# Dummy products from the start, activation tables regrouped in the first unit, and set-up writes moved, in a fused attention and gated feed-forward kernel

## The chip, the core and the metric

The kernel runs on one core of a Trainium2 chip. A core has TensorE (PE, matrix products into PSUM), VectorE (DVE), ScalarE (ACT, activation functions by tables), GpSimd (POOL) and SyncE (SP), and DMA queues. In this kernel GpSimd issues nearly all loads, and SyncE the stores. The metric is the device time of one execution in microseconds. Before the change it is 282.56 us, the median of three runs (282.09 to 282.75).

## What is computed

Two layers, one after the other. The first is an attention over 4 batches, 8 heads, 768 positions and head dimension 64, in which a query sees its neighbours nearer than 16 positions and one summary key for each block of 32:

```python
k_sum = k.reshape(B, H, nb, block, D).max(axis=3)
v_sum = v.reshape(B, H, nb, block, D).mean(axis=3)
scores_l = scale * np.matmul(q, k.transpose(0, 1, 3, 2))      # masked to |i - j| < 16
scores_s = scale * np.einsum('bhsd,bhnd->bhsn', q, k_sum) + np.log(block)
a = softmax(concatenate([scores_l_m, scores_s]))
x = a @ concatenate([v, v_sum])
```

The second layer takes x as 3072 tokens of 512, with d_ff = 1536:

```python
gelu = 0.5 * g * (1.0 + erf(g * inv_sqrt2))      # g = x @ w_gate
ffn_out = gelu * (x @ w_val) @ w_out
res_gate = 1.0 / (1.0 + np.exp(-(x @ w_res)))
out = x + res_gate * ffn_out
```

## The kernel before

**Units.** The work is cut into eight units (NU) of 384 tokens, two for each batch. For a unit, attention runs in four head pairs (hp):

- `s_step` (L268): 12 score products into the only buffer of the PSUM pool `ps_s`; exp on ScalarE (L280); a mask product on VectorE (L283), giving P.
- `av_step` (L286): 12 products of P with `vext` (v, and in partitions 96 to 127 the block means of v); a reciprocal and a product on VectorE give xn (L298, L300).
- `xt_step` (L302): three transposes on TensorE and a copy, giving xT (L307).

The feed-forward part of a unit follows:

- `fo_step` (L327), 12 times: four gate products (g) and four value products (vv) of 384 columns, gelu on ScalarE (L321), a product on VectorE giving gvT (L322). g and vv take PSUM buffers of `ps_mm`, which has four.
- `res_step` (L334), three times: four products of 512 columns and a tanh (L341).
- `ffn_step` (L343): 12 products of 512 columns for each of three sub-blocks, in pieces of four; `end_step` (L360) does two VectorE instructions (L354, L356) and the store.

While a unit's `res_step` and `ffn_step` run, the attention of the next unit is woven in by hand: `first_out` (L434) does it for unit 0, `mid_out` for the units after it. Each engine executes its instructions in the order in which the program lists them[...].

**Tables.** [...] Exp and tanh share one, gelu is in another; a load is put ahead of the activation that needs the other table. Copies need no change.

**The start.** `load_qk` (L85) brings k in two halves, `load_q` (L95) q, `v_loads` (L108) v in 12 windows, then the weights in pieces (L183 to L193), all by GpSimd in that order. VectorE writes constants in the meantime: `ident`, `maskt`, `bpair`, `bias_t`, `vext_consts`, `kw_consts`, `own_keys`, and `warm`, a tile of zeros. The program of unit 0 begins at L374. `k_step` turns k by 16 transposes for each head pair, copies it (L221) and takes block maxima on VectorE (`k_blocks`, L204). `q_step` (L228) turns q by eight transposes and a copy (L235). `vsum_mm` (L238) sums v over blocks with products of 256 columns that fill 32 columns of the array; the sums are cast (L392, L393) and copied into `vext` (`vsum_head`, L245). Then come the four `av_step`s and `xt_step`s of unit 0, with five dummy products between them (`keep_warm`, L403, a 128x128 by 512 product of zeros whose result nobody reads), and the first two gate and value products by hand (L418 to L431).

**Around L515.** In unit 0 the four `q_step`s of the batch's second half follow feed-forward steps 8 to 11. After step 10 the first score step of unit 1 is issued, whose exp falls on ScalarE between the gelus of steps 10 and 11.

The softmax here doesn't subtract the row's maximum and nothing guards it: scores larger than these inputs give would overflow.

## Time and profile before

| what | value |
|---|---|
| time | 282.56 us |
| span of the profiled execution | 281.2 us |
| TensorE busy | 260.4 us (93%) |
| VectorE busy | 163.5 us (58%) |
| ScalarE busy | 131.9 us (47%) |
| GpSimd busy | 103.3 us (37%) |
| gelu, 96 times | 47.0 us, 491 ns each |
| exp, 32 times | 28.8 us, 901 ns each |
| TensorE busy from 0 to 5, 5 to 10, 10 to 15 us | 0.00, 2.88, 3.92 us |
| TensorE busy from 40 to 45, 45 to 50 us | 4.29, 2.96 us |

Busy time is what an engine spent in instructions, not counting the issue of transfers. Products on TensorE overlap, and their ends are modelled, so its busy time is not its time at peak. The averages hide the stages. The last two rows of the table show what to look for: stretches in which the engine that is otherwise full stands still. An engine's idle time matters only where it lies on the chain of waits that ends last.

### The profile page before, as it was taken

To read this page: it belongs to the slowest core of one execution; us is meant where nothing else is said; L and a number is where in the kernel's file an instruction comes from. 1 tells how busy PE (TensorE), PEld (TensorE's weight loads), DVE (VectorE), ACT (ScalarE), POOL (GpSimd) and SP (SyncE) were. 2 spreads that over 40 slices of the span, in tenths; PEclk is the share of its full clock that TensorE was granted. 3 is DMA by queue.
4 is the path that set the end of the run, shared out by engine and by line. 5 is a ranking of instruction groups with operands and counts; after the bars stand their busy time and mean duration, and the time that the engine had idled before them with its cause. 6 is when DMAs were issued, how large, how long until landed. Compare 5 with 4: busy or idle time off the path is not lost.

```text
span 281.2 us, 5757 instructions
## 1 busy us (share of the span) xinstructions
PE 260.4 (93%) x2326; PEld 144.2 (51%) x2349; DVE 163.5 (58%) x366; ACT 131.9 (47%) x205; POOL 103.3 (37%) x130
## 2 busy tenths in 40 slices
PE   0799996999999999999899999999899999999994
PEld 0555553455555556455454555455455555456543
DVE  5965432489636734486866834575956733684424
ACT  1855549556473553652353434543254435444320
POOL 7995753600199982000899830000700000000000
PEclk9999999999999999999999999999999999999999
DMA  6999999991019999961099999421001100010003
GB/s 89 171 178 196 197 206 208 151 198 54 4 10 127 182 171 152 151 98 65 3 100 131 196 166 150 94 77 41 2 0 40 75 2 0 37 41 37 2 0 113
DMA packets 99818, 27.51 MB, mean 98 GB/s; under 512 B 83720, under 2 KB 96848, under 8 KB 99792
## 3 DMA queue, kind: packets, MB, share of 16 engines
q0 software_dynamic: 80560, 16.85, 68.4%
q1 hardware_dynamic: 19232, 10.30, 17.1%
q8 instruction: 18, 0.29, 0.4%
q14 instruction: 8, 0.07, 0.1%
HBM read 33.69 MB, written 6.29 MB: 142 GB/s over the span
## 4 chain that ended last, share of the span: by engine, by line
PE 83%; DVE 6%; ACT 4%; issue 3%; DMA 3%; POOL 0%; POOLq 0%; DVEq 0%
PE f L348 21%; PE g L316 20%; PE vv L316 19%; PE r L338 7%; PE ao L294 4%; PE s L276 3%; DMA q_sb<-in_q_dram 3%; PE xp L305 3%; DVE ks L207 2%; PE vs L241 2%; PE tp L233 2%; DVE gvT L322 2%; PE f L369 1%; ACT L280 1%; ACT L321 1%
## 5 line engine op out<-in xcount | busy, mean ns | idle before, releaser
L322 DVE TENSOR_TENSOR gvT<-ge,vv 128x384 bf16<-128x384 f32 x96 | 52.6, 552 | 58.9 <-PE vv L316 54.8
L321 ACT ACTIVATE ge<-g 128x384 f32<-128x384 f32 x96 | 47.0, 491 | 82.2 <-DVE gvT L322 43.7
L316 PE MATMUL vv<-xT,w_val 128*128 128x384 bf16 x384 | 78.4, 326 | 2.7 <-DVE gvT L322 2.7
L316 PE MATMUL g<-xT,w_gate 128*128 128x384 bf16 x384 | 79.9, 326 | 0.4 <-ACT ge L321 0.4
L348 PE MATMUL f<-w_out,gvT 128*128 128x512 bf16 x262 | 62.7, 379 | 1.4 <-issue 1.0
L316 PEld LDWEIGHTS <-w_val 128*128 128x128 bf16 x384 | 37.5, 98 | 28.7 <-issue 4.6
L316 PEld LDWEIGHTS <-w_gate 128*128 128x128 bf16 x384 | 35.8, 98 | 25.2 <-issue 3.0
L266 POOL COPY vext<-vsum 32x1536 bf16<-32x1536 bf16 x14 | 20.0, 1464 | 76.6 <-DMA vsum<-vpart 76.6
L280 ACT ACTIVATE P<-s,bias_t 128x768 bf16<-128x768 f32 x32 | 28.8, 901 | 30.6 <-PE s L276 30.5
L111 POOL DMA_DIRECT2D vext<-in_v_dram x48 | 36.5, 790 | 15.7 <-DMA w_out<-in_moe_w_out_dram 5.4
L348 PEld LDWEIGHTS <-gvT 128*128 128x128 bf16 x276 | 26.1, 98 | 29.1
L283 DVE TENSOR_TENSOR P<-P,maskt 128x768 bf16<-128x768 bf16 x32 | 17.7, 556 | 21.6 <-ACT P L280 21.6
L338 PE MATMUL r<-w_res,xT 128*128 128x512 bf16 x88 | 23.9, 381 | 0.4
L354 DVE SCALAR_TENSOR_TENSOR th<-th,f 128x512 f32<-128x512 f32 (+1 forms) x25 | 16.5, 659 | 6.4 <-PE f L348 6.1
L300 DVE TENSOR_TENSOR xn<-ao,rz 128x384 bf16<-128x384 f32 x32 | 17.8, 558 | 1.1
L119 POOL DMA_DIRECT2D k_nat<-in_k_dram x24 | 18.1, 771 | 0.0
L356 DVE SCALAR_TENSOR_TENSOR o<-th,xn 128x512 f32<-128x512 f32 (+1 forms) x25 | 16.8, 671 | 0.9
L298 DVE RECIPROCAL rz<-ao 128x6 f32<-128x6 f32 x32 | 6.2, 193 | 17.7 <-PE ao L294 17.7
L294 PEld LDWEIGHTS <-P 128*64 128x64 bf16 x384 | 9.0, 115 | 14.1 <-DVE P L283 5.5
L341 ACT ACTIVATE th<-r 128x512 f32<-128x512 f32 x24 | 14.2, 595 | 3.3 <-PE r L338 2.9
L207 DVE TENSOR_REDUCE ks<-kW 128x24 bf16<-128x768 bf16 x16 | 15.2, 948 | 0.3
L276 PE MATMUL s<-qT,kW 64*128 64x64 bf16 x384 | 11.8, 197 | 2.7 <-ACT P L280 2.7
(69 smaller groups left out, 188.4 us busy)
## 6 DMA issues: line engine op xcount, KB each, us to landing
out_dram<-o SPq DMA_DIRECT2D x23, 256.0 KB
vext<-in_v_dram POOLq DMA_DIRECT2D x40, 96.0 KB, 6.0
k_nat<-in_k_dram POOLq DMA_DIRECT2D x20, 96.0 KB, 3.7
q_sb<-in_q_dram POOLq DMA_DIRECT2D x4, 384.0 KB, 7.3
w_gate<-in_moe_w_gate_dram POOLq DMA_DIRECT2D x6, 256.0 KB, 8.2
w_val<-in_moe_w_val_dram POOLq DMA_DIRECT2D x6, 256.0 KB, 9.3
w_out<-in_moe_w_out_dram POOLq DMA_DIRECT2D x3, 512.0 KB, 14.3
q_nat<-in_q_dram POOLq DMA_DIRECT2D x12, 128.0 KB, 5.2
```

What stands on the lines that cost most here:

```text
L111: nc.gpsimd.dma_start(out=vext[b % 2][r0:r1, t, :, 0:D], in_=src)
L119: nc.gpsimd.dma_start(out=k_nat[r0:r0 + hi - lo, t].rearrange("p (h d) -> p h d", d=D), in_=k[b, :, lo:hi, :].rearrange("h p d -> p h d"))
L207: nc.vector.tensor_reduce(out=ks.rearrange("d (t n) -> d t n", n=2), in_=kw[:, :, WIN:WIN + QT].rearrange("d t (n w) -> d t n w", w=BLK), ...
L266: eng.tensor_copy(vext[b % 2][96:128, lo:hi, :, 0:D], src)
L276: nc.tensor.matmul(s[:, hh, t * QT:(t + 1) * QT], kw[ps, tt, hp, :], qt[ps, tt // 2, hp, (tt % 2) * QT:(tt % 2 + 1) * QT], start=True, sto ...
L280: nc.scalar.activation(P.rearrange("p a t q -> p a (t q)"), s[:, :, 0:TU], AF.Exp, scale=scale, bias=bias_t[:])
L294: nc.tensor.matmul(ao[64 * e:64 * e + 64, sub, hh, :], P[:, hh, t, :], vext[b % 2][:, half * HT + t, 2 * hp + hh, 0:D + 1], start=True, st ...
L316: nc.tensor.matmul(ps[:, 0:TU], w[:, ko, fo * 128:(fo + 1) * 128], st["xT"][:, ko, :], start=(ko == 0), stop=(ko == KO - 1), skip_group_ch ...
L321: nc.scalar.activation(ge[:], g[:, 0:TU], AF.Gelu)
L322: nc.vector.tensor_mul(gvT[:, fo, :], ge[:], vv[:, 0:TU])
L338: nc.tensor.matmul(r[:], st["xT"][:, ko, ss], w_res[:, ko, :], start=(ko == 0), stop=(ko == KO - 1))
L348: nc.tensor.matmul(st["f", sub][:], gvT[:, fo, ss], w_out[:, fo, :], start=(fo == 0), stop=(fo == FO - 1), skip_group_check=True)
```

## The change

It has four parts.

1. `keep_warm` now takes its buffer from `ps_s` and is called before any data has come (12 products), and three more times among the turns of k and q (3, 4 and 2). The memset of `warm` becomes VectorE's first instruction. The purpose is to have TensorE's clock up when the first real products come.
2. A gelu of one element (`gate1`) follows the fourth exp of unit 0. It has no use but to have the gelu table loaded there, and not at the first real gelu.
3. The score step of unit 1 after feed-forward step 10 is gone; `first_out` does it itself, and its order is new, so that no exp stands between gelus.
4. The constants for the second buffers (`vsum[1]`, `bgrp`, the ends of `k_nat`, `kW[1]`) are written after unit 0's attention and not at the start.

```diff
+    gate1 = const.tile([1, 1], F32, name="gate1")
...
+        nc.vector.memset(warm[:], 0.0)
         nc.vector.memset(ident[:], 0.0)
...
         own_keys(bmat, NT)
-        nc.vector.memset(warm[:], 0.0)
         vext_consts(1)
-        nc.vector.memset(vsum[1][96:128, :], 0.0)
-        own_keys(bgrp, 3)
-        nc.vector.memset(k_nat[0:32, 0], 0.0)
-        nc.vector.memset(k_nat[64:96, NT - 1], 0.0)
-        kw_consts(1)
...
-        for hp in range(3):
-            k_step(0, hp, ps_mm, "mm")
+        def keep_warm(n):
+            wp = ps_s.tile([128, 2, 512], F32, tag="s", name="wp")
+            for _ in range(n):
+                nc.tensor.matmul(wp[:, 0], warm[:, 0:128], warm[:], start=True, stop=True)
+
+        keep_warm(12)
+        k_step(0, 0, ps_mm, "mm")
+        k_step(0, 1, ps_mm, "mm")
+        keep_warm(3)
+        k_step(0, 2, ps_mm, "mm")
         tp3 = turn_pair(k_sb[0], 3, ps_mm, "mm")
+        keep_warm(4)
         q_step(0, 0, 0, ps_mm, "mm")
         k_place(0, 3, tp3)
+        keep_warm(2)
         q_step(0, 0, 1, ps_mm, "mm")
...
         s_step(0, 3, st)
+        nc.scalar.activation(gate1[:], bias_t[0:1, :], AF.Gelu)
         vsum_mm(0, vs, 8, NT)
...
         xt_step(0, 2, st, ps_t, "t", nc.scalar.copy)
+        nc.vector.memset(vsum[1][96:128, :], 0.0)
+        own_keys(bgrp, 3)
+        nc.vector.memset(k_nat[0:32, 0], 0.0)
+        nc.vector.memset(k_nat[64:96, NT - 1], 0.0)
+        kw_consts(1)
...
         def first_out(u, st, gvT, nst):
-            s_step(n, 1, nst)
+            s_step(n, 0, nst)
             res_step(st, 0)
             res_step(st, 1)
+            ffn_step(st, gvT, 0, 0, 4)
+            ffn_step(st, gvT, 1, 0, 4)
             av_step(n, 0, nst)
+            s_step(n, 1, nst)
+            res_step(st, 2)
+            ffn_step(st, gvT, 2, 0, 4)
+            ffn_step(st, gvT, 0, 4, 8)
+            av_step(n, 1, nst)
             s_step(n, 2, nst)
-            res_step(st, 2)
-            for sub in range(NSUB):
-                ffn_step(st, gvT, sub, 0, 4)
-            av_step(n, 1, nst)
+            xt_step(n, 0, nst, **turn)
+            ffn_step(st, gvT, 1, 4, 8)
+            ffn_step(st, gvT, 2, 4, 8)
+            av_step(n, 2, nst)
             s_step(n, 3, nst)
-            xt_step(n, 0, nst, **turn)
-            ffn_step(st, gvT, 0, 4, 8)
-            ffn_step(st, gvT, 1, 4, 8)
-            av_step(n, 2, nst)
             xt_step(n, 1, nst, **turn)
-            ffn_step(st, gvT, 2, 4, 8)
+            ffn_step(st, gvT, 0, 8, FO)
+            end_step(u, st, 0)
+            ffn_step(st, gvT, 1, 8, FO)
             av_step(n, 3, nst)
             xt_step(n, 2, nst, **turn)
-            ffn_step(st, gvT, 0, 8, FO)
-            end_step(u, st, 0)
+            ffn_step(st, gvT, 2, 8, FO)
             xt_step(n, 3, nst, **turn)
-            ffn_step(st, gvT, 1, 8, FO)
             end_step(u, st, 1)
-            ffn_step(st, gvT, 2, 8, FO)
             end_step(u, st, 2)
...
-                if u == 0 and fo == 10:
-                    nst = new_unit()
-                    s_step(1, 0, nst)
```

## The prediction

> **What bounds the kernel now.** First the summary of the chain that ended last, for the engine that carries the span; then that chain in order of time, to find where TensorE does not carry it; then the timeline there. The summary:

> ```profile
> PE 83%; DVE 6%; ACT 4%; issue 3%; DMA 3%; POOL 0%; POOLq 0%; DVEq 0%
> ```

> TensorE's own work is 83% of the chain. So a gain comes only from making its products shorter, or from closing its gaps. Both occur before 61 us; from then on the change touches nothing. The front, from the chain in order of time (start, duration, what):

> ```profile
> 3.18 7.39 DMA q_sb<-in_q_dram
> ...
> 13.15 1.39 PE vs L241 x6
> ...
> 18.66 1.62 PE vs L241 x7
> 20.28 0.02 issue
> 20.30 0.44 DVE vsum L392
> ...
> 21.55 0.54 PE ao L294 x12
> ...
> 27.53 1.28 ACT L321
> ```

> The reader sees the wait for q (to 10.57 us), then TensorE with slow products: six vs products of 256 columns take 1.39 us, 0.23 each; the last is ScalarE's table load ahead of the first gelu. That they are slow shows in the same twelve ao products further on, here in the chain of 38 to 62 us:

> ```profile
> 42.85 1.28 ACT L280
> ...
> 45.06 1.28 ACT L321
> ...
> 47.23 1.28 ACT L280
> ...
> 49.48 0.35 PE s L276 x12
> ...
> 53.39 0.31 PE ao L294 x12
> ```

> ao takes 0.54 us early and 0.31 us later: TensorE is at half speed early. In the timeline ao still takes 0.54 at 24.33 us and 0.42 at 25.23, so the change of speed falls near 25.4. (The page's PEclk row shows full speed throughout; here the durations decide.) The three loads above are the second place: exp, gelu, exp in turn, each switch 1.28 us, while TensorE idles. The table by stretches prices it (us, then PE, PEld, DVE, ACT, POOL busy, then clock and transfers):

> ```profile
> 42.30:50.80 8.50, 5.75 (x78) 3.21 (x78) 2.71 (x6) 8.36 (x11) 2.31 (x3) 1.00 1.40 199
> 60.40:70.00 9.60, 9.35 (x106) 5.16 (x104) 9.20 (x22) 6.35 (x10) 0.00 (x0) 1.00 0.48 119
> ```

> In the first stretch ScalarE is full (8.36 of 8.50) and TensorE lacks 2.75 us. In the second, the start of unit 1, VectorE is nearly full as well: a gain must reach VectorE there, not only TensorE.

> [...] TensorE had work with small pauses from 11.7 to 20.3 us and stayed slow[...]; the early work is transposes, 64-row scores and vs products that fill 32 columns. [...] here the next activation starts 0.01 us after the load[...].

> **The change part by part.** Times are in us from the start.

> *Dummies before data.* The memset of warm is now VectorE's first; it takes 0.27 from 0.89, so TensorE starts near 1.2. Twelve products cost 12 x 0.43 = 5.1 at most and end by 6.3; k lands at 6.42. Hidden at either speed. Three more stand before the third k turn (0.65 warm), whose data lands at 8.62; turns of the first half end by 7.9, sooner if warm. Four (0.86) stand before the first q turn: k turns end near 9.7, so they end at 10.55, q lands at 10.57. Two (0.43) stand where TensorE waited 0.57 for ScalarE's copy. All hidden if warm; if cold they are not (rivals).

> *Scores and vs.* q0's copy starts at about 10.95 in place of 11.19, then ScalarE has 0.48 + 0.96 + 0.48 of copies, so exp 0 starts near 12.9 as before (12.79). The exps then stood at 15.01, 16.87 and 18.70, because cold vs products lie between. Warm, the step is set by ScalarE: exp 0.90 + q copy 0.48 + 0.05, about 1.43; exp 3 runs from 17.2 to 18.1. But vs also needs v. Its last load is issued at 13.87 (timeline) and takes 4.5 to land (the first line below): 18.4. So vs ends at about 18.7, not at 20.28: **1.6 gained**, where halving all products would promise more.

> *Table load in the pause.* Load and gate run from 18.1 to about 19.6 (1.28[...]). That delays ScalarE's vsum cast by 0.9. Queued behind it are the two copies for heads 4 to 7 (1.56 together), done by 21.6; the third and fourth ao need them at 21.9 and 22.7. Hidden. VectorE's copies feed the first two ao's.

> *ao and turns.* Before, vs end to first ao was 1.27; kept, it starts at 19.95. From there to the last turn took 5.12 (21.55 to 26.67), in which VectorE idled 0.65 and 0.54 for cold products. Warm, it is VectorE's 4 x (0.20 + 0.56 + 0.03) = 3.15 plus 0.3 + 0.2: 3.65. **1.45 gained**.

> *No load at the first gelu.* The load lasted 1.28, but TensorE stood still only 0.42 (before 29.36), having four PSUM buffers to fill: **0.42 gained**. Together 3.5: the third gate product starts near 25.9.

> *Consts spread.* About 1.8 us of VectorE memsets leave 7.4 to 9.05. They delayed k placement, but q sets the first score, so I cost this at nothing. They return after the last xn (23.6 to 25.4), ahead of the first gvT product, whose gelu ends near 25.4. Nothing either.

> The view of transfers, asked around single issues, gives KB and us from issue to landing of the last v window, the last w_gate piece and the first w_out piece:

> ```profile
> vext<-in_v_dram POOLq DMA_DIRECT2D x1, 80.0 KB, 4.5
> ...
> w_gate<-in_moe_w_gate_dram POOLq DMA_DIRECT2D x1, 256.0 KB, 11.7
> ...
> w_out<-in_moe_w_out_dram POOLq DMA_DIRECT2D x1, 512.0 KB, 14.2
> ```

> *fo loop.* 0.65 per four products, unchanged, if weights are there. Landing times are issue plus time to landing: last w_gate piece 24.12 + 11.7 = 35.8, last w_val 37.2, second q 34.4. Needed, with 3.5 less: 37.0, 37.7, 35.0. All just fit; a front gain over 4 would wait for transfers. Without the early score (0.28) the loop and its q turns end at 44.22 - 3.5 - 0.3 = 40.4.

> *first_out.* Work on TensorE: 48 products of 512 columns x 0.216 = 10.4; four scores 1.2; four ao 1.24; four turns 1.1: 13.9, ending at 54.4. Does it wait? w_res lands at 39.7, w_out at 42.3, 44.8, 47.4; first needed at 40.7, then 42.5, 46.5, 51. Exp 0: copy to 41, load to 42.2, exp to 43.1, mask to 43.7; its ao comes at 44.2. No wait, the first w_out by 0.2. Before, 44.22 to 60.77 was 16.55; now 14.0, and 0.28 moved in: about 2.3 to 2.6. VectorE limits it: last xn to about 54.3, two output pairs of 1.38, so its first gvT comes near 57.1 against 62.89. ScalarE's gelu load, behind the last turn's copy, allows it at 57.0. So **5.8 in all** at unit 1, of which 2.3 from here. The stretch after it is relative to itself; its k landed at 51.1. I take off 0.2 for waits of a few hundredths: 5.6, or 282.56 - 5.6 = 277.0.

> **Rivals.**
> - The clock falls back in the score and vs stretch (11 to 19), where no dummy stands and the work resembles what failed to raise it. For: the 11.7 to 20.3 stretch of before. Against: from 45 to 50 TensorE was busy 2.96 of 5 us and stayed fast, so keeping may need less than raising. vs then ends near 18.9 to 19.2, ao and turns keep their 5.12; the front gains about 1.7 with the table: 4.0 in all, 278.6.
> - first_out becomes bound by transfers: the first w_out has 0.2 of slack, the second q 0.6. For: transfers run steadily near 200 GB/s and are not sped up. Against: they do not slow either. Half the second gain and 1 us of the first are lost: about 3.4, 279.2.
> - Dummies run cold and lie on the path: the third k turn waits 0.6, four cold dummies end at 12.4 instead of 10.6, two more take 0.86: 2.3 to 2.7 lost at the front, 0.4 won at the table. If first_out also pays only half (1.2), 283.4, slower than before; if it pays all, about 282.5.

> **How the numbers follow.** 60% for the forecast (276.2 to 277.9, since hidden terms are good to 0.8), 23% for the fallen clock, 9% for transfers, 8% for cold dummies (6 slower, 2 same). The range 275.9 to 279.4 takes in the first two and most of the third. Faster 0.92, same 0.02, slower 0.06.

> **What would show it.** Right: twelve ao near 0.31 at about 20; vs ending near 18.7 with the last v's landing before it; no load at the first gelu; one load between gelus and exps near 41; the first gate product of unit 1 at 54 to 55. Wrong: ao of 0.54, q turned after 11, TensorE waiting on w_out, or VectorE late into unit 1.

## The result and the profile after

The changed kernel takes 279.99 us (median of four runs, 279.03 to 280.02) against 282.32 us (281.94 to 282.75) for the kernel before on the same chip: a ratio of 0.9909, interval 0.9882 to 0.9935. It is faster by 2.3 us. The forecast was 5.6.

The summary of the chain that ended last, read in the same order as before:

```profile
PE 83%; DVE 6%; DMA 5%; issue 2%; ACT 1%; POOL 1%; POOLq 0%; DVEq 0%
```

ScalarE's share fell from 4% to 1%, and transfers rose from 3% to 5%. So a transfer wait has come in. The chain in order of time (start, duration, what) names it:

```profile
3.19 7.31 DMA q_sb<-in_q_dram
...
12.30 6.58 DMA vext<-in_v_dram
18.89 0.04 issue
18.93 1.44 PE vs L237 x6
...
52.94 0.31 PE ao L290 x12
...
58.02 1.28 ACT L317
```

A window of v, issued at 12.30, is waited for until 18.88. It is the tenth of the twelve (window 9). After it six vs products take 1.44, or 0.24 each, as slow as before the change. The last line is one table load at 58.02; the three at 42.85, 45.06 and 47.23 are gone. (A load takes 1.28 throughout; there are 18 in the trace of before and 16 here. But for the first, at 0.81, each stands between an exp or a tanh and a gelu, ahead of the exp or the gelu. A copy has none, nor has a tanh, after an exp or, in before at 267.67, after a gelu.) TensorE's timeline has the place of the damage (start, duration, line, operation, tiles, shape, count; in brackets the wait ahead of it and what ended it):

```profile
15.13 0.61 PE L237 MATMUL vs<-vext,bmat 96*32 96x256 bf16 x4
...
17.47 0.38 PE L237 MATMUL vs<-vext,bmat 96*32 96x256 bf16 x2 [1.72 <-DMA vext<-in_v_dram]
17.78 0.50 PE L272 MATMUL s<-qT,kW 64*128 64x64 bf16 x12
...
21.26 0.54 PE L290 MATMUL ao<-vext,P 128*64 128x65 bf16 x12
...
24.79 0.38 PE L290 MATMUL ao<-vext,P 128*64 128x65 bf16 x12
```

The first line is at full speed (four vs in 0.61). Then TensorE stands still for 1.72 us for window 7 of v. Right after this wait the fourth score takes 0.50, where a fast one takes 0.35, and the first ao takes 0.54 at 21.26 and 0.38 at 24.79. The trace's records of the clock say the same: full speed from 4.08, half from 17.73, full again from 24.56. The table by stretches shows it (us, then busy time of PE, PEld, DVE, ACT, POOL, the granted clock, transfers):

```profile
15.20:18.60 3.40, 1.68 (x21) 1.05 (x21) 0.75 (x2) 1.18 (x2) 2.51 (x5) 0.87 2.12 166
18.60:22.00 3.40, 3.29 (x23) 1.35 (x21) 2.12 (x5) 3.32 (x6) 3.40 (x5) 0.50 1.46 196
22.00:25.40 3.40, 3.17 (x45) 1.64 (x43) 2.10 (x7) 1.68 (x3) 2.14 (x4) 0.62 1.45 196
...
42.30:50.80 8.50, 8.50 (x100) 4.18 (x98) 2.52 (x6) 5.63 (x8) 2.32 (x3) 1.00 1.40 197
...
60.40:70.00 9.60, 9.12 (x101) 4.90 (x99) 8.96 (x22) 5.19 (x9) 0.00 (x0) 1.00 0.64 120
```

TensorE is busy 1.68 of 3.40 us around the wait; the next stretch runs at clock 0.50, and there it looks full (3.29) because its products are slow. The fourth row answers to the second gap of before: 8.50 busy of 8.50, where it was 5.75. The fifth, the start of unit 1, differs little from before.

Two landmarks split the gain. The third gate product starts at 28.49 instead of 29.36: 0.87 won at the front, where 3.5 was forecast. The first gvT of unit 1 starts at 59.83 instead of 62.89, which is 3.06 in all, so 2.19 comes from the new `first_out`, where 2.3 was forecast. Nearly the whole shortfall lies ahead of 29 us.

### The profile page after: what moved, and what is told of

The parts are those of the page before. It is cut to its first block, busy times and chain, and to the rows that moved or that the text cites. A ratio compares the mean times of both kernels' runs of the same rounds, so it can differ in the third digit from the quotient of the medians.

```text
span 278.3 us, 5822 instructions
## 1 busy us (share of the span) xinstructions
PE 265.1 (95%) x2370; PEld 143.4 (52%) x2370; DVE 163.3 (59%) x366; ACT 129.8 (47%) x204; POOL 103.5 (37%) x130
## 3 DMA queue, kind: packets, MB, share of 16 engines
q1 hardware_dynamic: 19232, 10.30, 18.4%
## 4 chain that ended last, share of the span: by engine, by line
PE 83%; DVE 6%; DMA 5%; issue 2%; ACT 1%; POOL 1%; POOLq 0%; DVEq 0%
PE g L312 21%; PE f L344 21%; PE vv L312 20%; PE r L334 8%; PE ao L290 4%; PE s L272 3%; DMA q_sb<-in_q_dram 3%; PE xp L301 2%; DMA vext<-in_v_dram 2%; DVE ks L203 2%; DVE gvT L318 2%; PE tp L229 1%; PE f L365 1%; PE wp L373 1%; PE vs L250 1%
## 5 line engine op out<-in xcount | busy, mean ns | idle before, releaser
L344 PE MATMUL f<-w_out,gvT 128*128 128x512 bf16 x276 | 65.5, 379 | 0.0
L276 ACT ACTIVATE P<-s,bias_t 128x768 bf16<-128x768 f32 x32 | 28.9, 902 | 31.9 <-PE s L272 31.7
L120 POOL DMA_DIRECT2D k_nat<-in_k_dram x24 | 18.1, 768 | 0.0
L294 DVE RECIPROCAL rz<-ao 128x6 f32<-128x6 f32 x32 | 6.2, 192 | 17.2 <-PE ao L290 17.2
L337 ACT ACTIVATE th<-r 128x512 f32<-128x512 f32 x24 | 14.2, 595 | 3.4 <-PE r L334 2.9
L290 PE MATMUL ao<-vext,P 128*64 128x65 bf16 x384 | 12.6, 203 | 0.0
## 6 DMA issues: line engine op xcount, KB each, us to landing
out_dram<-o SPq DMA_DIRECT2D x23, 256.0 KB
w_gate<-in_moe_w_gate_dram POOLq DMA_DIRECT2D x6, 256.0 KB, 8.1
w_val<-in_moe_w_val_dram POOLq DMA_DIRECT2D x6, 256.0 KB, 8.7
w_out<-in_moe_w_out_dram POOLq DMA_DIRECT2D x3, 512.0 KB, 14.7
```

What stands on the lines that cost most here:

```text
L120: nc.gpsimd.dma_start(out=k_nat[r0:r0 + hi - lo, t].rearrange("p (h d) -> p h d", d=D), in_=k[b, :, lo:hi, :].rearrange("h p d -> p h d"))
L276: nc.scalar.activation(P.rearrange("p a t q -> p a (t q)"), s[:, :, 0:TU], AF.Exp, scale=scale, bias=bias_t[:])
L290: nc.tensor.matmul(ao[64 * e:64 * e + 64, sub, hh, :], P[:, hh, t, :], vext[b % 2][:, half * HT + t, 2 * hp + hh, 0:D + 1], start=True, st ...
L344: nc.tensor.matmul(st["f", sub][:], gvT[:, fo, ss], w_out[:, fo, :], start=(fo == 0), stop=(fo == FO - 1), skip_group_check=True)
```

## The experiments

Two questions stood open: what lets the clock fall at 17.73, and why v comes late. For the first, one theory is the wait itself, an idle stretch of 1.7 us. Its rival is the one already in the prediction, that the thin products between 11 and 19 us cannot hold the clock whether TensorE waits or not. Each run is compared with runs of the kernel before on its own chip.

**The four parts undone one by one.**

```diff
 # undo_dummies
-        keep_warm(12)
...
-        keep_warm(3)
...
-        keep_warm(4)
...
-        keep_warm(2)
```

> The changed kernel without its 21 early dummy products (12, 3, 4 and 2); all else as changed. Theory A (the wait): TensorE waits for a v window from 15.7 to 17.5 us, this lets the clock fall at 17.7 and eats most of what the early clock won, so undoing the dummies costs little: 280.0 to 280.5, with vs ending near 20.3 as in the kernel before. Rival C (the early clock alone made the front's 0.7 us and more, hidden by the gate's load on ScalarE): 281 or more, with the third gate product at or after 29.4.

279.44 us (279.34 to 280.11), ratio 0.9878 [0.9851, 0.9905]. It is no slower than the changed kernel, measured again below at 279.88 (279.68 to 280.10). Its clock rises once, at 22.63. As long as the wait for v stands, the early dummies are worth nothing that can be measured.

```diff
 # undo_order: the old first_out, and in the feed-forward loop
+                if u == 0 and fo == 10:
+                    nst = new_unit()
+                    s_step(1, 0, nst)
```

> The changed kernel with the old order: the score step after feed-forward step 10 and the old first_out. The page of after gives this part 2.1 us (q turns of unit 0 end 1.0 earlier than before, unit 1's first gvT product 3.06 earlier). If that reading holds: 279.99 + 2.1 = 282.1, with three table loads between 41 and 47. Rival: much of it comes from other orders and the early score hides work; then under 281.

282.78 us (280.98 to 283.97 in 14 runs), ratio 0.9991 [0.9966, 1.0015]. By the median the new order is worth 2.9, as much as the whole gain. But the 14 runs form two groups of seven, near 281.8 and 283.6, so it is worth 1.9 in one and 3.7 in the other. The chain of the profiled run, one of the slower group, shows what the old order does:

```profile
41.89 1.28 ACT L276
...
44.11 1.28 ACT L317
...
46.28 1.28 ACT L276
...
48.88 1.82 PE r L334 x4
...
50.70 3.41 PE f L344 x12
```

The three loads are back. And after them the four r products take 1.82 and the twelve f products 3.41, where the trace of before has

```profile
49.83 0.97 PE r L338 x4
50.80 2.59 PE f L348 x12
```

In this run the clock was at half from 48.81 to 52.23. A part of the price of the old order is a second fall of the clock, in some runs. The granted clock separates the two groups: 0.980 or 0.981 over the whole span in the slower seven, 0.987 to 0.992 in the others.

```diff
 # undo_gate
-        nc.scalar.activation(gate1[:], bias_t[0:1, :], AF.Gelu)
```

> The changed kernel without the one-element gelu: the table load returns to the first gelu. The forecast's step gave the load 0.42 us of TensorE's time: 280.4, the same or less where it is hidden by four full PSUM buffers. Rival: the gate's load delays ScalarE's vsum cast (20.76, where vs ended at 20.37) and so costs what it wins: 280.0.

280.33 us (280.11 to 280.79), ratio 0.9914 [0.9894, 0.9934]: 0.45 slower than the changed kernel. The forecast for this part was 0.42. The difference is small: the fastest of these runs (280.11) stands next to the slowest of the changed kernel (280.10).

```diff
 # undo_consts: back at the start, and gone after the third xt_step
         vext_consts(1)
+        nc.vector.memset(vsum[1][96:128, :], 0.0)
+        own_keys(bgrp, 3)
+        nc.vector.memset(k_nat[0:32, 0], 0.0)
+        nc.vector.memset(k_nat[64:96, NT - 1], 0.0)
+        kw_consts(1)
```

> The changed kernel with the constants of the second buffers written at the start again. Forecast: hidden, 280.0. Rival: VectorE's placement of k is then late by 0.8 to 1 us, the first score with it, and ScalarE's exps: up to 0.5 more, 280.5.

279.72 us (279.06 to 279.89), ratio 0.9886 [0.9864, 0.9908]. No difference from the changed kernel, as forecast.

The changed kernel itself, once more:

> The changed kernel itself, so that the other runs have it beside them: 280.0 by its four runs. If the wait for v is what lets the clock fall, its trace shows TensorE idle ahead of the vs product of window 7, and then ao at 0.54 us.

279.88 us, ratio 0.9896 [0.9873, 0.9920]. Its clock is at half from 18.90 to 25.73.

**Is it the wait or the thin products?** Two runs, one without the wait and one with other products in it.

```diff
 # no_v_wait, in vsum_mm: windows 5 to 11 read window 4, which has landed
-                                     vext[b % 2][0:BAND, t, 4 * i:4 * i + 4, 0:D],
+                                     vext[b % 2][0:BAND, min(t, 4), 4 * i:4 * i + 4, 0:D],
```

> The changed kernel in which the block sums of v for unit 0's batch are taken from windows 0 to 4 where they should be from windows 5 to 11 (so the sums differ): no vs product waits for a late v load, the work on TensorE is the same. Theory A (the wait): the clock does not fall at 17.7; vs ends near 17.5, ao takes 0.31, and the front gains what was forecast and more: 3 us, 277.0, or less where weights then bound the loop. Rival B (thin products: transposes, 64-row scores and 32-column vs do not hold the clock): the clock falls all the same, ao takes 0.54 us, vs ends near 18.5, the gain is 1 to 1.8 us: 278.2 to 279.

277.05 us (276.86 to 277.55), ratio 0.9791 [0.9762, 0.9819]. This kernel leaves out the true sums of windows 5 to 11; the work on TensorE is the same. The clock stays full from 5.15 to the end:

```profile
15.20:18.60 3.40, 2.55 (x28) 1.51 (x26) 1.94 (x5) 2.94 (x3) 2.89 (x5) 1.00 2.14 168
18.60:22.00 3.40, 2.61 (x57) 1.80 (x57) 2.67 (x8) 2.86 (x7) 3.31 (x6) 1.00 1.45 196
```

TensorE is idle for 0.85 us of the first row and stays at 1.00. The timeline shows what the row holds:

```profile
16.34 1.05 PE L237 MATMUL vs<-vext,bmat 96*32 96x256 bf16 x8
17.40 0.59 PE L373 MATMUL wp<-warm 128*128 128x512 bf16 x2
19.31 0.38 PE L290 MATMUL ao<-vext,P 128*64 128x65 bf16 x12 [1.31 <-ACT vsum L400]
```

From 11.23 to 17.40 TensorE has nothing but thin products (transposes, scores, vs), with pauses of 0.46, 0.16 and 0.23, and the clock holds. So the rival falls as it was put: thin products with pauses of no more than 0.46 held the clock here. And one long wait did not bring it down: the clock stayed up through the one of 1.31 us after 17.99, which has two dummies (wp) ahead of it.

```diff
 # fill: fill(n) is n products of warm
-        vsum_mm(0, vs, 5, 8)
+        vsum_mm(0, vs, 5, 7)
+        fill(8)
+        vsum_mm(0, vs, 7, 8)
...
-        vsum_mm(0, vs, 8, NT)
+        vsum_mm(0, vs, 8, 9)
+        fill(3)
+        vsum_mm(0, vs, 9, 10)
+        fill(2)
+        vsum_mm(0, vs, 10, NT)
```

> The changed kernel with 13 more dummy products of 512 columns where TensorE waits for v: 8 ahead of vs of window 7, 3 ahead of window 9, 2 ahead of window 10; nothing else. Theory A (the wait): the clock stays up, ao takes 0.31 us, vs ends with the last v landing near 19.5, the first ao at 20.7, the turns gain 1.45: 1.8 to 2.3 us in all, 277.7 to 278.2. Rival B (thin products): the clock falls before the dummies or in spite of them, and these cost double: 279.5 to 281.

278.92 us (278.87 to 279.17), ratio 0.9854 [0.9827, 0.9882]. Here v comes as late as ever, but the clock holds:

```profile
15.20:18.60 3.40, 3.40 (x32) 1.53 (x30) 0.78 (x2) 1.25 (x3) 3.09 (x5) 1.00 2.16 167
18.60:22.00 3.40, 3.13 (x26) 1.12 (x25) 1.88 (x5) 3.28 (x6) 3.36 (x6) 1.00 1.45 196
```

With 1.72 us of wait among the same thin products the clock fell; with eight dummies in the wait it held. With the wait filled 1.0 us comes back. The other 1.9, up to `no_v_wait`, has two parts that this run does not separate. One is the late v itself: the fourth score and exp stand behind it in TensorE's order (in the changed kernel window 7's product starts at 17.47, the score at 17.78, its exp at 18.32). The other is the dummies: window 7, issued at 10.80, landed after 6.1, at 16.9, and its product starts at 17.54, behind the eight of them.

```diff
 # no_v_no_dum: no_v_wait without the four early keep_warm calls
```

> The kernel of no_v_wait (block sums of unit 0's batch from windows 0 to 4 in place of 5 to 11, so the sums differ) without the 21 early dummies. With the wait for v the dummies were worth -0.4 us. If they are worth something only where no wait eats it: slow vs products end near 20.0 again, 279.3 to 279.6, so 2.3 to 2.5 us for the dummies. Rival (they are worth nothing even then): 277.0 to 277.5.

279.76 us (279.30 to 280.02), ratio 0.9891 [0.9858, 0.9923]. Against `no_v_wait` the early dummies are worth 2.7 us. The part of the change that measured nothing with the wait is worth about as much, without it, as the new order.

```diff
 # s3_first: the last score goes ahead of the windows that are late
-        vsum_mm(0, vs, 5, 8)
+        vsum_mm(0, vs, 5, 7)
         s_step(0, 3, st)
...
-        vsum_mm(0, vs, 8, NT)
+        fill(4)
+        vsum_mm(0, vs, 7, 9)
+        fill(3)
+        vsum_mm(0, vs, 9, 10)
+        fill(2)
+        vsum_mm(0, vs, 10, NT)
```

> The kernel with the 13 filling products, and the fourth score step moved ahead of the vs products of windows 7 and 8 (dummies: 4 ahead of window 7, 3 ahead of 9, 2 ahead of 10), so that it doesn't stand behind the wait for v: exp 3 starts near 16.6 where it was 18.25, and the gelu table is there by 18.8. If the last v window sets the end of vs (20.0 to 20.5), the time stays as with the filling alone, 278.9; if ScalarE's late load and casts set it, 278.2 to 278.5.

278.64 us (278.50 to 278.76), ratio 0.9853 [0.9829, 0.9876], with the clock full to the end. It takes the exp out of the wait, but the cast of the sums still starts at 20.13, against 20.19 in the changed kernel. TensorE waits for no window here: the last one, issued at 13.82, landed after 5.4, near 19.2, and its products start at 19.59, behind two dummies. So v and the dummies set this end together.

**Why is v late?** The prediction took its landing from the trace of before, with nothing in the change that touches the transfer. An attempt to take the sums from another, wider load:

```diff
 # v_wide
-        v_loads(0)
+        v_sb = k_nat.rearrange("p t f -> p (t f)")[:, 0:H * PJ * D].rearrange("p (h j d) -> p h j d", h=H, j=PJ)
+        nc.gpsimd.dma_start(out=v_sb.rearrange("p h j d -> p h (j d)"),
+                            in_=v[0].rearrange("h (p j) d -> p h (j d)", j=PJ))
+        v_loads(0, range(HT))
...
 # ahead of the third piece of w_out
+            if c == 2:
+                v_loads(0, range(HT, NT))
...
 # lo, hi: 0 to 4 in place of the vs of windows 0 to 2, 4 to 8 in place of the next
+            for j in range(lo, hi):
+                nc.tensor.matmul(vs[96:128, :], bsum[:], v_sb[:, :, j, :], start=(j == 0), stop=(j == PJ - 1))
```

> The changed kernel with the block sums of v taken from one load of v in long packets (8 consecutive positions a partition, eight products of 512 columns in place of 24 of 256, summed over 4 partitions), issued after q; then only windows 0 to 5 of v, which unit 0 reads; windows 6 to 11 go between the second and third w_out piece; VectorE makes all four head copies, and bmat is gone. Theory A (v's landing is the front's bound, directly and by the clock): vs ends near 15, the first ao comes at 17.5 to 18.5 when window 5 has landed, the clock holds, the loop is then bound by weights or not at all: 276.0 to 277.5. Rival (the other loads only move: the same bytes must land ahead of w_out): 278.5 to 279.5, with TensorE waiting on w_val or w_out.

282.05 us (281.31 to 283.46), ratio 0.9985 [0.9970, 0.9999]: a miss. Its load landed at 14.04, 8.74 after issue, and TensorE waited for it. TensorE's waits, in us, times and the longest:

```profile
PE vs L401 <- DMA k_nat<-in_v_dram: 2.0, 1, 2.0
```

The clock fell at 13.79 and came back at 27.44. The wait was moved, not removed.

The other thing the change does to v is where it lands. `gate1` is one number of 4 bytes, but it takes 32 bytes in each partition, and all tiles allocated after it (kW, qT, vext, the weights) move up by 32 bytes; vext from address 74240, a multiple of 64, to 74272.

```diff
 # no_gate_tile
-    gate1 = const.tile([1, 1], F32, name="gate1")
...
-        nc.scalar.activation(gate1[:], bias_t[0:1, :], AF.Gelu)
+        nc.scalar.activation(vpart[0:1, 0:1], bias_t[0:1, :], AF.Gelu)
 # before_shift, in the kernel before
     warm = const.tile([128, 512], BF16, name="warm")
+    spacer = const.tile([1, 1], F32, name="spacer")
...
+        nc.vector.memset(spacer[:], 0.0)
```

> The changed kernel, with the one-element gelu writing into a corner of vpart (not in use then) and the new tile gate1 gone. gate1 takes 32 bytes of each partition, so every tile after it (kW, qT, vext, the weights) began 32 bytes later than before; now they begin where they did in the kernel before, at multiples of 64. Theory D (the shift slows v's short writes): the last v window takes 4.5 to 4.8 us again and window 7 4.7 to 4.8, TensorE hardly waits ahead of window 7, the clock holds, 277.5 to 278.5. Rival E (something else in the change delays v, such as the fetch of instructions at another moment): 5.3 or more, clock lost near 18, 279.9.

> The kernel before with a tile of one element after warm (and a memset of it), which shifts all later tiles by 32 bytes as gate1 does; nothing else. Theory D: window 7 of v takes 6.0 or more to land, the last 5.3 or more; the time changes little, as slow vs products hide it: 282.5 to 283.2. Rival E: 4.7 and 4.5 to 4.8 as in the two traces of before.

> The kernel before, for a second trace of v's landing. In the first the last v window took 4.5 us and window 7 4.8; in the traces with the change 5.3 to 5.9 and 6.0 to 6.8. If the change itself delays them, 4.5 and 4.8 again; if it varies from run to run, 5.3 or more, and then the forecast rested on one early landing.

The view of the tile vext, for the five loads of v issued between 10.5 and 14.6 us, gives the time from issue to landing (least, median, most). The lines are those of before, before_again, before_shift, the changed kernel, after_again and no_gate_tile, in this order:

```profile
DMA to landing us min/median/max: 4.5/4.8/5.2
```

```profile
DMA to landing us min/median/max: 4.7/5.1/5.5
```

```profile
DMA to landing us min/median/max: 5.2/5.7/6.0
```

```profile
DMA to landing us min/median/max: 5.6/6.6/6.7
```

```profile
DMA to landing us min/median/max: 5.4/6.0/6.2
```

```profile
DMA to landing us min/median/max: 4.6/4.9/5.3
```

With the extra tile the median is 5.7 to 6.6; without it 4.8 to 5.1. The other runs with gate1 agree (undo_dummies 6.1, undo_gate 6.7, undo_consts 6.3). The kernel before, with nothing added but the spacer and its memset, has the late landing too. So the extra tile is the cause, and not the faster TensorE. The late landing costs that kernel no time (282.41, ratio 0.9999 [0.9987, 1.0012]): its slow vs products reach the windows later than v does. The seven loads of v ahead of these five hardly differ: their medians are 5.6 to 6.1 without the tile and 6.0 to 6.2 with it.

`no_gate_tile` takes 278.57 us (277.14 to 279.05), ratio 0.9844 [0.9817, 0.9871]: 1.3 less than after_again, for moving one number to another tile. (The two ran on different chips; their ratios' intervals do not overlap.) In one of its six runs the granted clock was 1.00, and that one took 277.14; the other five had 0.994 or less and took 278.35 to 279.05. In the trace, one of the five, the clock falls at 18.8 for 3.41 us:

```profile
18.60:22.00 3.40, 3.22 (x31) 1.13 (x31) 2.15 (x5) 2.59 (x5) 3.36 (x5) 0.53 1.45 196
```

Ahead of that stand four waits for v of 0.34, 0.19, 0.22 and 0.24: 0.99 in all. In before_again, the kernel before once more (282.92), the clock is at half from 48.21 for 3.41 us, in the pause between the table loads.

**Two versions with v on time.**

```diff
 # s3_no_gate_tile: s3_first and no_gate_tile together
```

> The kernel of s3_first (fourth score step ahead of the waiting vs products, 9 more dummies there) without the tile gate1. Theory D: vs ends near 19.2 in place of 20.1, 277.5 to 277.9, the best version. Rival E: 278.6 as s3_first.

279.11 us (278.16 to 280.21), in two groups near 278.3 and 280.0; ratio 0.9870 [0.9839, 0.9901]. A miss: no better than either alone. In the profiled run, one of the slower group, the clock falls at 16.68, as the fourth score ends; the third and the fourth score had waited 0.16 and 0.45 for the exps. The timeline shows the dummies right after it, here and, second, in `s3_first`, where three of the four are recorded, in 0.81:

```profile
16.70 1.89 PE L377 MATMUL wp<-warm 128*128 128x512 bf16 x4
```

```profile
16.70 0.81 PE L378 MATMUL wp<-warm 128*128 128x512 bf16 x3 [0.16 <-issue]
```

A dummy that comes after the pauses comes too late in this run. In `s3_first` the same pauses did not bring the clock down.

```diff
 # small_fill: no_gate_tile, with seven dummies among the windows
         vsum_mm(0, vs, 0, 3)
+        fill(2)
...
-        vsum_mm(0, vs, 5, 8)
+        vsum_mm(0, vs, 5, 7)
+        fill(2)
+        vsum_mm(0, vs, 7, 8)
...
-        vsum_mm(0, vs, 8, NT)
+        for t in range(8, NT):
+            vsum_mm(0, vs, t, t + 1)
+            if t < NT - 1:
+                fill(1)
```

> The changed kernel without the tile gate1 and with 7 small dummies in the pauses of the score and vs stretch: 2 after vs of windows 0 to 2 (a pause of 0.46), 2 ahead of window 7 (0.34), 1 ahead of windows 9, 10 and 11 (0.2 each). Theory: v lands early (4.6 to 4.8), [...] the clock stays up from about 5 us to the end in every execution, vs ends near 18.8 and ao takes 0.31: 277.0 to 277.6, what was forecast. If the clock still falls in some executions (thin products with pauses are at the edge whatever is added), two groups of times, 277.2 and 278.5; if the dummies lie on the path, 278.5 in all.

277.43 us (277.35 to 277.53), ratio 0.9797 [0.9768, 0.9825]: the best of the versions that sum all of v, and some 2.5 under the changed kernel. The clock is full from 5.99 to the end:

```profile
15.20:18.60 3.40, 3.24 (x37) 1.34 (x29) 1.43 (x3) 2.53 (x4) 3.40 (x6) 1.00 2.09 171
18.60:22.00 3.40, 3.09 (x48) 1.50 (x47) 2.44 (x7) 2.92 (x6) 3.28 (x5) 1.00 1.45 196
```

## Why the prediction was wrong at the front and right behind it

- **Dummies before data: right as placed, worth less.** That twelve would bring the clock up was the author's estimate. It was recorded at full speed from 4.08, 2.82 after the first of them. They took 4.14 us, from 1.26 to 5.40: up to 3.80 they start 0.40 to 0.43 apart, from 4.16 on 0.22. So the forecast's 0.43 and 0.216 a product were right; q was turned at 10.54 (forecast 10.55) with nothing delayed. But of a clock raised at 4 us nothing was left at 17.73.
- **Scores and vs: the step that failed.** It said of the last v load that it "takes 4.5 to land: 18.4. So vs ends at about 18.7, not at 20.28: **1.6 gained**". The landing was read off the kernel before and taken as fixed. In the changed kernel the last load took 5.6, and the four ahead of it up to 6.7. The cast that follows vs started at 20.19 instead of 20.30: 0.11 gained for 1.6. The prediction also checked the last window alone. TensorE waited ahead of window 7, the eighth of twelve, with the last score behind it, and exp 3 started at 18.32 where 17.2 was forecast. (Without the wait, in `no_v_wait`, it starts at 16.45: ScalarE's sum was about 0.75 too long, and so the need for window 7 came earlier than the forecast had it.) After the wait the clock fell, at 17.73, and the last six vs products took 0.24 each. With the last landing near 19.4 and two products of window 11 at full speed (0.39), vs would have ended near 19.8, an estimate: so about 1.1 of the 1.6 went with the landing, the rest with the slow products.
- **ao and turns: fell with it.** "**1.45 gained**" rests on fast products from 20 us on. The clock was at half from 17.73 to 24.56, ao took 0.54 and the step about 5.1, as before. In `small_fill` the cast starts at 19.18 and the first ao at 20.10 (forecast 19.95), and the third gate product at 26.04 (forecast 25.9).
- **Gate: right.** 0.45 measured for 0.42. The load took 1.28 and the gelu of one number 0.20, where 0.2 was the author's estimate. What the prediction missed is that its output is a tile, and that the tile moves others. With `no_gate_tile` at 278.57 this cost 1.3, about three times what the gate itself earns.
- **Consts: right**, nothing. **first_out: right**, 2.19 by the landmarks for 2.3. Undoing it costs 1.9 in the runs without a second fall of the clock and 3.7 in those with one, a price that the forecast did not have. TensorE waited for no weights there, so the transfer rival is out.
- **The fallen clock as a rival.** The prediction gave it 23% with 278.6. That the clock falls in this stretch was right. The cause was half right: the products are thin, but the clock fell where TensorE also waited. The size was wrong: it kept 0.4 for the table and 1.3 for vs, and the second was lost to v. Its argument against, that from 45 to 50 us TensorE "was busy 2.96 of 5 us and stayed fast", rests on one execution. In before_again and in before_shift the clock fell there, at 48.21 and 49.12. Of the 93 runs of the kernel before that stand beside the experiments, 70 had a granted clock of 0.997 or more, and 23 had 0.992 to 0.994, as these two traces (0.992 and 0.993); the 23 took 282.95 us or more, the 70 no more than 282.92.
- **The sum.** Forecast 3.5 at the front, of which 0.87 came; without the two faults (the late v and the fall of the clock), in `small_fill`, 3.32 of it comes, and the first gvT of unit 1 starts at 57.39, where 57.1 was forecast. Of the 2.45 us between the changed kernel and `small_fill`, 1.3 came back when the tile went and 1.1 more with seven dummies in the waits that were left. The working was sound for a v that lands as before and a TensorE that does not stand still. The changed kernel gives neither, and even with the tile gone the clock fell in five of six runs.

Open is which of the moved tiles matters, and by what a place 32 bytes off makes the landing later; no run moved vext alone. The traces' transfers narrow it: the 8500th of v's 8960 packets ends at 17.05 in before and in the changed kernel, the last at 18.14 and at 19.01, so only the last few hundred are late. Open too is when the clock falls: the last section gives what these few traces show.

## What to carry to other kernels

A faster engine meets the next transfer: before counting a speed-up, list for every load in the stretch when it lands and when the faster engine will ask for it, in its order, and not only for the last one. Look for the waits that remain before adding dummy products: here the 21 early ones measured nothing as long as the wait for v stood, and 2.7 us without it; seven more in the waits that were left brought 1.1. And look at what a new tile does to the addresses of the old ones: here moving them by 32 bytes went with a landing later by 0.6 us or more, and writing the one number into a tile that existed took 1.3 us off.
